# Row sums of a hash attention: the first three key tiles summed by transfers instead of GpSimd, with a new order of the work around them

## The chip, the cores and the metric

One core of a Trainium2 chip. The metric is the time of one launch on the device in microseconds (us), as the median of several runs. A program on one core has no second core to compare with, so a run's state is judged by its distance from the fastest run of the same kernel. Ratios are the mean time of one kernel's fast runs over that of the kernel before in the same rounds, with a 95% interval, so not quite the ratio of the medians quoted beside them.

Engines: PE is TensorE (matmuls; PEld its weight loads), DVE VectorE, ACT ScalarE, POOL GpSimd, SP SyncE, which issues most transfers. `L694` is line 694 of the kernel.

## The reference, cut to what matters

```python
q, k, v: (4, 8, 768, 64) float32        # batch, heads, sequence, head dimension
q_bits = einsum(q, proj) > 0             # 6 hash bits a row, the same for k
mask   = bucket(q_bits)[..., :, None] == bucket(k_bits)[..., None, :]
scores = where(mask, q @ k.T / 8, -1e9)
attn   = exp(scores - max);  attn = attn / (attn.sum(-1) + 1e-9)
x      = (attn @ v) as (3072, 512)
h      = x @ w_in                        # 512 -> 2048
out    = (max(h, 0) + alpha * min(h, 0)) @ w_out      # 2048 -> 512
```

The argument is about `attn.sum(-1)`, the row sums.

## The kernel before

Attention is done in 32 units: 16 pairs of heads, two halves of 384 queries each. A unit has six key tiles; for each, PE makes the scores transposed (keys on partitions), ACT takes the exponential into a tile `p(u, kc)` of 128 x 2 x 384 floats, and PE multiplies it with v. The sum over keys is a sum over the six tiles, then over partitions: GpSimd adds tiles 0, 1 and 2 to `accp`, DVE adds tiles 3, 4, 5 and `accp` to `accd`, and a matmul with ones (`totals`) sums `accd` over the partitions, for DVE to divide by. In the same 32 units, DVE pre-processes the weights of the feed-forward part.

```python
    def add_first(u):
        accp[u] = pool.tile([P, 2, CW], F32, name=f"accp{u}", tag="accp")
        do(POOL.tensor_tensor(accp[u], p(u, 0), p(u, 1), op=ALU.add))

    def add_third(u):
        do(POOL.tensor_tensor(accp[u], accp[u], p(u, 2), op=ALU.add))

    def add_last(u):
        accd[u] = pool.tile([P, 2, CW], F32, name=f"accd{u}", tag="accd", bufs=1)
        do(DVE.tensor_tensor(accd[u], p(u, 3), p(u, 4), op=ALU.add))
        do(DVE.tensor_tensor(accd[u], accd[u], p(u, 5), op=ALU.add))
        do(DVE.tensor_tensor(accd[u], accd[u], accp[u], op=ALU.add))
    ...
    for u in range(UNITS):
        scores(u, 0)                 # key tiles 0 and 1
        add_first(u)
        if u > 0:
            add_last(u - 1)
        ...                          # first turn (transposes of q) or first half of the hashes
        if u > 0:
            attend(u - 1, 0)
        weight_parts(u)
        scores(u, 1)                 # key tiles 2 and 3
        add_third(u)
        weight_sum(u)
        weight_group(u)              # in every 4th (later every 2nd) unit: four sums and their stores
        ...                          # second turn (k), or second half of the hashes
        if u > 0:
            attend(u - 1, 1)
            totals(u - 1)
        scores(u, 2)                 # key tiles 4 and 5
        if u > 0:
            divide(u - 1)
        ...                          # loads; at u == 16 also x loads and GpSimd's four subtractions
```

`do` keeps the written order on each engine.

## Time and profile before

| | before |
|---|---|
| time, median of the runs told with the changed kernel | 997.8 us (997.5 to 998.2) |
| attention stage, to the start of its last exponential | 400.7 us |
| two undisturbed units | 23.62 us |

The prediction below shows the page's head and reads it. The groups of the sum (columns: line, engine, operation, out<-in, forms, count, then busy us, mean ns of one, idle time before and who ended it):

```profile
L667 POOL TENSOR_TENSOR accp<-pt,pt 128x768 f32<-128x768 f32 x32 | 62.0, 1939 | 222.5 <-ACT pt L658 185.2
...
L670 POOL TENSOR_TENSOR accp<-accp,pt 128x768 f32<-128x768 f32 x32 | 62.3, 1946 | 39.0 <-ACT pt L658 38.9
...
L676 DVE TENSOR_TENSOR accd<-accd,accp 128x768 f32<-128x768 f32 x32 | 53.4, 1667 | 3.3
...
L675 DVE TENSOR_TENSOR accd<-accd,pt 128x768 f32<-128x768 f32 x32 | 43.7, 1364 | 3.3
L674 DVE TENSOR_TENSOR accd<-pt,pt 128x768 f32<-128x768 f32 x32 | 40.3, 1260 | 0.0
```

The GpSimd additions are 62.0 + 62.3 us, 1.94 us each. The three DVE additions do the same amount of work each and should take the same time; they differ (1260, 1364, 1667 ns) because they are held up.

### The profile page before, as it was taken

What the parts mean: (1) busy time and instruction counts of PE and PEld (TensorE: products, weight loads), DVE (VectorE), ACT (ScalarE), POOL (GpSimd) and SP (SyncE); (2) the same over time, 40 slices, a digit from 0 to 9 for tenths busy, and PEclk for the clock granted to TensorE, in tenths of its full rate; (3) what the DMA queues carried; (4) which work ended last, traced back from release to release, by engine and by line L of the source; (5) the groups of instructions that cost most, each with busy time, mean ns of one, the idle gap of its engine ahead of it and who ended that gap; (6) DMA issues with size and microseconds to landing.
All of it is one profiled execution on the core that took longest, in us unless ns stands there. A gap on an engine that the chain in (4) does not pass through costs nothing.

```text
span 998.3 us, 12489 instructions
## 1 busy us (share of the span) xinstructions
PE 963.2 (96%) x4741; PEld 594.0 (60%) x4741; DVE 605.8 (61%) x959; ACT 371.0 (37%) x669; POOL 158.5 (16%) x98
## 2 busy tenths in 40 slices
PE   6999999989999998999999999999999999999997
PEld 3444444434444443455788655888656888556886
DVE  3999999999999999766600366500467300665100
ACT  6777676665777664222100122100222000222000
POOL 2333333262333333000300000300000300000000
PEclk9999999998999999999999999999999999999999
DMA  7465756355444431463400133300224200231000
GB/s 199 126 182 143 237 154 179 107 164 157 143 143 143 127 111 53 200 259 110 137 22 22 58 111 99 123 22 21 71 88 155 68 22 22 84 111 37 22 22 24
DMA packets 93316, 106.81 MB, mean 107 GB/s; under 512 B 53296, under 2 KB 79936, under 8 KB 93248
## 3 DMA queue, kind: packets, MB, share of 16 engines
q1 hardware_dynamic: 91680, 105.54, 33.1%
q8 instruction: 39, 0.64, 0.3%
q10 hardware_dynamic: 1568, 0.39, 0.2%
q14 instruction: 29, 0.24, 0.1%
HBM read 78.65 MB, written 27.26 MB: 106 GB/s over the span
## 4 chain that ended last, share of the span: by engine, by line
PE 61%; DVE 35%; ACT 1%; issue 1%; DMA 1%; DVEq 0%; SPq 0%; ACTq 0%
PE z_2a L756 6%; PE z_1a L756 6%; PE z_0a L756 6%; DVE accd L676 5%; DVE accd L675 4%; DVE accd L674 4%; DVE wx L553 3%; PE z_1c L756 3%; PE z_0c L756 3%; PE z_2c L756 3%; DVE wr L577 2%; DVE wr L557 2%; PE f_2a L756 2%; PE f_3a L756 2%; PE f_7a L756 2%; PE f_6a L756 2%
## 5 line engine op out<-in xcount | busy, mean ns | idle before, releaser
L658 ACT ACTIVATE pt<-sc 128x768 f32<-128x768 f32 x192 | 149.9, 813 | 119.8 <-PE sc L653 119.8
L653 PE MATMUL sc<-qT,kT 64*128 64x384 f32 x768 | 157.5, 487 | 0.0
L686 PE MATMUL av<-pt,vn 128*64 128x385 f32 (+1 forms) x768 | 138.1, 495 | 0.0
L667 POOL TENSOR_TENSOR accp<-pt,pt 128x768 f32<-128x768 f32 x32 | 62.0, 1939 | 222.5 <-ACT pt L658 185.2
L686 PEld LDWEIGHTS av<-pt,vn 128*64 128x64 f32 x768 | 49.4, 136 | 72.6 <-issue 72.6
L732 POOL TENSOR_TENSOR x<-x,x 128x768 f32<-128x768 f32 x16 | 31.9, 2005 | 364.0 <-DMA x<-x_s 363.4
L810 DVE TENSOR_TENSOR g<-g,g 128x384 f32<-128x384 f32 x128 | 82.5, 665 | 2.2
L653 PEld LDWEIGHTS sc<-qT,kT 64*128 64x128 f32 x768 | 69.8, 190 | 15.3 <-issue 15.2
L653 PEld LDWEIGHTS <-kb 64*128 64x128 bf16 x384 | 24.4, 94 | 79.3 <-issue 62.7
L653 PE MATMUL sc<-qb,kb 64*128 64x384 bf16 x384 | 64.6, 329 | 5.6 <-ACT pt L658 5.6
L670 POOL TENSOR_TENSOR accp<-accp,pt 128x768 f32<-128x768 f32 x32 | 62.3, 1946 | 39.0 <-ACT pt L658 38.9
L756 PE MATMUL z_2a<-wo,g 128*128 128x256 f32 x256 | 58.0, 379 | 0.5 <-ACT z_2u L763 0.5
L756 PE MATMUL z_1a<-wo,g 128*128 128x256 f32 x256 | 57.9, 379 | 0.0
L756 PE MATMUL z_0a<-wo,g 128*128 128x256 f32 x256 | 57.9, 379 | 0.0
L676 DVE TENSOR_TENSOR accd<-accd,accp 128x768 f32<-128x768 f32 x32 | 53.4, 1667 | 3.3
L803 DVE SCALAR_TENSOR_TENSOR g<-h,alpha 128x384 f32<-128x384 f32 x32 | 22.1, 692 | 54.4 <-ACT h L795 54.4
L756 PEld LDWEIGHTS z_2a<-wo,g 128*128 128x128 f32 x256 | 48.6, 190 | 8.1 <-ACT z_2u L763 0.9
L756 PEld LDWEIGHTS z_0a<-wo,g 128*128 128x128 f32 x256 | 48.6, 190 | 7.5
L756 PEld LDWEIGHTS z_1a<-wo,g 128*128 128x128 f32 x256 | 48.6, 190 | 6.6
L675 DVE TENSOR_TENSOR accd<-accd,pt 128x768 f32<-128x768 f32 x32 | 43.7, 1364 | 3.3
L674 DVE TENSOR_TENSOR accd<-pt,pt 128x768 f32<-128x768 f32 x32 | 40.3, 1260 | 0.0
L639 ACT ACTIVATE qb<-hs,hb 32x384 bf16<-32x384 f32 x64 | 36.7, 574 | 2.2 <-PE hs L636 1.0
(217 smaller groups left out, 1477.1 us busy)
## 6 DMA issues: line engine op xcount, KB each, us to landing
wi<-w_in_s SPq DMA_DIRECT2D x32, 896.0 KB, 4.6
raw<-in_moe_w_in_dram SPq DMA_DIRECT2D x16, 512.0 KB, 4.1
raw<-in_moe_w_out_dram SPq DMA_DIRECT2D x16, 512.0 KB, 3.6
w_in_s<-wsi SPq DMA_DIRECT2D x16, 448.0 KB, 5.4
w_out_s<-wso SPq DMA_DIRECT2D x8, 896.0 KB, 4.4
wo<-w_out_s SPq DMA_DIRECT2D x8, 896.0 KB, 7.4
qn<-in_q_dram SPq DMA_DIRECT2D x32, 192.0 KB, 3.7
vn<-in_v_dram SPq DMA_DIRECT2D x16, 384.0 KB, 4.4
```

The source lines that it names most:

```text
L639: do(ACT.activation(bits["q", pi][D * s : D * s + 32, cols], ps[r], AF.Sign, bias=hb[r]))
L653: do(PE.matmul(sc[:, s, :CW], what["k", pi][r, ks], what["q", pi][r, qs], start=first, stop=not first,))
L658: do(ACT.activation(pt[:, :, :CW], sc[:, :, :CW], AF.Exp, scale=SCALE / DOWN))
L667: do(POOL.tensor_tensor(accp[u], p(u, 0), p(u, 1), op=ALU.add))
L670: do(POOL.tensor_tensor(accp[u], accp[u], p(u, 2), op=ALU.add))
L674: do(DVE.tensor_tensor(accd[u], p(u, 3), p(u, 4), op=ALU.add))
L675: do(DVE.tensor_tensor(accd[u], accd[u], p(u, 5), op=ALU.add))
L676: do(DVE.tensor_tensor(accd[u], accd[u], accp[u], op=ALU.add))
L686: do(PE.matmul(av[u][D * s : D * s + D, :w], nat["v", pi][:, s, kc * D : (kc + 1) * D], prob[u, kc][:, s, :w], start=(kc == 0), stop=(kc = ...
L732: do(POOL.tensor_tensor(x_m[b, to], x_m[b, a], x_m[b, c], op=ALU.subtract))
L756: do(PE.matmul(self.ps[bank], self.left(left, k), self.right(right, k), start=start and k == 0, stop=k == self.nk - 1, skip_group_check=no ...
L810: do(DVE.tensor_tensor(g_m[to, i], g_m[x, i], g_m[y, i], op=op))
```

## The change

Its intent: get the additions off GpSimd, since they hold DVE up, by letting transfers do them. A transfer copies tile 0 into `accp`, two more, issued from GpSimd, add tiles 1 and 2 on the way. The rest makes room and time: DVE's addition of `accp` is moved behind the first weight operations of the next unit, weight sums are made one (later two) to a unit instead of four at once, and the second turn is moved behind the last scores.

```diff
     def weight_group(i):
         ...
-        for to, a, c in sums4:
-            do(DVE.tensor_tensor(w[:, to], w[:, a], w[:, c], op=ALU.subtract))
-        ... stores
+        for x in sums4:
+            sums_due.append((one, x))
+        sums_due.append((store, ()))      # weight_sums(n) makes n of them
     def add_first(u):
         accp[u] = pool.tile([P, 2, CW], F32, name=f"accp{u}", tag="accp")
-        do(POOL.tensor_tensor(accp[u], p(u, 0), p(u, 1), op=ALU.add))
+        nc.sync.dma_start(accp[u], p(u, 0))
+        nc.gpsimd.dma_start(accp[u], p(u, 1), accum_op=ALU.add)
     def add_third(u):
-        do(POOL.tensor_tensor(accp[u], accp[u], p(u, 2), op=ALU.add))
+        nc.gpsimd.dma_start(accp[u], p(u, 2), accum_op=ALU.add)
     def add_last(u):
         ...
+    def add_total(u):
         do(DVE.tensor_tensor(accd[u], accd[u], accp[u], op=ALU.add))
@@ the loop over units
         weight_parts(u)
+        if u > 0:
+            add_total(u - 1)
         scores(u, 1)
         add_third(u)
         weight_sum(u)
+        weight_sums(1 if u < HW else 2)
         weight_group(u)
-        (second turn of k, or second half of the hashes)
         if u > 0:
             attend(u - 1, 1)
             totals(u - 1)
         scores(u, 2)
         if u > 0:
             divide(u - 1)
+        (second turn of k, or second half of the hashes)
-        if u == HW:                       # HW is 16: x loads, GpSimd's four subtractions
+        if u == HW + 2:
```

More of the change, by code (lines that the diff above doesn't have):

```diff
@@ L584, in weight_sum @@
         ))
+    sums_due = []
     def weight_group(i):
@@ L597, in weight_group, with one, store, weight_sums @@
             return
-        for to, a, c in sums4:
+        def one(to, a, c):
             do(DVE.tensor_tensor(w[:, to], w[:, a], w[:, c], op=ALU.subtract))
-        if i < HW:
-            c, kk = divmod(n, 2)
-            for ii in range(4):
-                nc.sync.dma_start(w_in_s[4 * c + ii][:, :, kk], w[:, :, ii])
-        else:
-            nc.sync.dma_start(w_out_s[n], w)
+        def store():
+            if i < HW:
+                c, kk = divmod(n, 2)
+                for ii in range(4):
+                    nc.sync.dma_start(w_in_s[4 * c + ii][:, :, kk], w[:, :, ii])
+            else:
+                nc.sync.dma_start(w_out_s[n], w)
+        for x in sums4:
+            sums_due.append((one, x))
+        sums_due.append((store, ()))
+    def weight_sums(count):
+        while sums_due and (count or sums_due[0][0].__name__ == "store"):
+            fn, x = sums_due.pop(0)
+            count -= fn.__name__ == "one"
+            fn(*x)
     def turn(pi, name, half):
@@ L893, in fast_path @@
         weight_sum(u)
+        weight_sums(1 if u < HW else 2)
         weight_group(u)
-        if more:
-            if g == 0:
-                turn(pi + 1, "k", 0)
-                turn(pi + 1, "k", 1)
-            else:
-                hash_bits(pi + 1, 1)
         if u > 0:
@@ L908, in fast_path @@
             divide(u - 1)
+        if more:
+            if g == 0:
+                turn(pi + 1, "k", 0)
+                turn(pi + 1, "k", 1)
+            else:
+                hash_bits(pi + 1, 1)
         load_weight(u + 3)
-        if u == HW:
+        if u == HW + 2:
             load_w(0)
@@ L928, in fast_path @@
     add_last(last)
+    add_total(last)
     attend(last, 1)
@@ L932, in fast_path @@
     divide(last)
+    weight_sums(4)
     attn.close()
```

## The prediction

> **What bounds the kernel now.** I read the page first (span, busy shares, the 40 slices), then the chain of waits, then PE's list of waits over the attention stage, then the timeline of two units in it, then a table of short stretches.
>
> ```profile
> span 998.3 us, 12489 instructions
> PE 963.2 (96%) x4741; PEld 594.0 (60%) x4741; DVE 605.8 (61%) x959; ACT 371.0 (37%) x669; POOL 158.5 (16%) x98
> ...
> PE   6999999989999998999999999999999999999997
> ...
> DVE  3999999999999999766600366500467300665100
> ...
> PE 61%; DVE 35%; ACT 1%; issue 1%; DMA 1%; DVEq 0%; SPq 0%; ACTq 0%
> ```
>
> Two stages: attention fills the first 16 slices (to about 402 us), the feed-forward part the rest. In the second stage PE is full and DVE is half idle, and the change doesn't touch its matmuls. In the first both PE and DVE stand at nines, and the chain's 35% of DVE lies there almost alone. So the question is which of the two sets the pace. PE's waits from 18 to 410 us answer it:
>
> ```profile
> PE sm L698 <- DVE accd L676: 7.7, 6, 3.0
> PE sc L653 <- ACT pt L658: 5.6, 31, 0.4
> PE tp_q L614 <- DVE st L708: 2.7, 6, 0.6
> PE tp_k L614 <- ACT qT L615: 1.3, 1, 1.3
> PE hs L636 <- DVE st L708: 0.4, 1, 0.4
> ```
>
> In all 17.7 us of 392. PE is the bound even here, and DVE is nearly level with it: it stops PE in a few units only. Units are 32; the starts of the scores that open a unit in the timeline (128.81, 140.63, 152.45) are 11.82 us apart, and in that unit PE's rows follow each other without a gap but for one of 0.17 before those scores. All periods taken that way are 11.8 except: three of about 12.6 in the first half, each after a unit that makes four weight sums; five of 12.2 to 12.6 in the second half (303.22 to 315.82, for example), also by units with four sums; and one of 17.75.
>
> Why DVE is so full is seen in the timeline:
>
> ```profile
> 120.44 0.96 DVE L675 TENSOR_TENSOR accd<-accd,pt 128x768 f32<-128x768 f32 x1
> ...
> 120.64 2.44 POOL L667 TENSOR_TENSOR accp<-pt,pt 128x768 f32<-128x768 f32 x1 [6.32 <-ACT pt L658]
> ...
> 121.51 2.39 DVE L676 TENSOR_TENSOR accd<-accd,accp 128x768 f32<-128x768 f32 x1
> ```
>
> The same addition of 128x768 takes DVE 0.96 us alone and 2.39 beside a GpSimd addition. The groups say the same: accd rows mean 1260, 1364 and 1667 ns, the shift (L553) 1149 ns where it takes 430 alone.
>
> The 17.75 us unit:
>
> ```profile
> 210.37 8.39 POOL L732 TENSOR_TENSOR x<-x,x 128x768 f32<-128x768 f32 x4
> ...
> 212.68 2.19 DVE L557 SCALAR_TENSOR_TENSOR wr<-raw,wr 128x512 f32<-128x512 uint32 x1
> ...
> 225.84 1.55 PE L698 MATMUL sm<-accd,ones 128*64 128x384 f32 x4 [3.04 <-DVE accd L676]
> ```
>
> and the stretch after it (columns: PE, PEld, DVE, ACT, POOL busy, PEclk, DMA share, GB/s):
>
> ```profile
> 226.00:232.00 6.00, 6.00 (x22) 2.72 (x23) 5.66 (x14) 2.00 (x3) 0.00 (x0) 0.50 0.30 74
> ```
>
> Four GpSimd subtractions in a row hold four DVE operations at about 2.2 us where they take 0.7 (0.43 one of them): 6 us lost. PE then waits 3.4 us, and the last row (PEclk 0.50) shows it at half clock for the next 6 us or more, about 3 us more.
>
> **What the Trainium skill says.**
> 1. "SBUF — State Buffer", Who interferes with whom: GpSimd's only SBUF ports are DVE's second pair; a DVE operation with two SBUF inputs, or in a two-port mode, and a GpSimd operation that reads SBUF exclude each other for a whole instruction. The trace agrees: 0.96 against 2.39 us.
> 2. "DMA: Bandwidth & Descriptors", SWDGE vs HWDGE vs iDMA: a transfer that adds can be issued from GpSimd only, whose cores write the descriptors. Its Anatomy of one DMA puts some 2 us fixed on each. No adding transfer is in this trace; plain ones land after 3.1 (192 KB) to 4.4 us (384 KB), which fits.
> 3. "Collectives: The Full Stack", The bandwidth ceiling: an adding transfer reads two sources and so ran at half a copy's rate. No run shows it here yet.
> 4. "TensorE: Matmul & The Clock Gate", What's actually happening: the clock is halved after an idle window, judged in free-running windows of about 3.4 us. The half clock after the 3.04 us wait agrees; after a wait of 2.06 us at 384 there was none, so the phase matters.
>
> **The change part by part.**
> *GpSimd additions out.* 64 of them, 124 us busy, leave GpSimd; DVE loses what they held it up. By rows that ran alone, in start-to-start distances, a unit needs of DVE: three additions 3.15, five weight operations on 128x512 and the reduction 3.8, division 2.3, one weight sum 0.7 (two small ones 0.9), together 10.0 to 10.3 us. Against PE's 11.8 this is 1.5 to 1.8 us of room where there was none. The gain is not these microseconds of DVE, only PE's waits that they caused.
> *Weight sums spread.* One per unit (two small ones in the second half) in place of four at once. With the room above, the long periods go: 3 x 0.8 + about 3.6 in the second half = 6.0 us.
> *Second turn behind the scores.* Two transposes of k, or the second half of the hashes (0.8 us of PE), now lie between the last scores of a unit and the first of the next. The 0.17 us wait for the exponential of two tiles back is then covered: up to 31 x 0.17 = 5.3, of which I count 5.0. It also brings the sums' matmul 0.8 us earlier, and ACT does the copies ahead of the first exponentials: these come some 0.3 to 0.9 us later. No matmul is added or removed.
> *Loads and GpSimd subtractions two units later.* The 8.4 us of lock stay. With DVE's lead over the sums' matmul still about 2.2 us, PE waits some 3 us again; only the two GpSimd additions right after are gone. I count 2 us of the 6.
> *The end.* The last two units have no turns, so PE needs only about 10.1 us each; before, it waited 2.06 (384 us), 1.21 (397) and 1.09 (408). DVE is no longer late there, but the transfers have less time. I count 1 us.
> *Transfers added.* Per unit one copy of 393 KB and two additions of 393 KB onto it, one after another. DMA load: 256 packets of 1536 B at about 72 ns is 18 engine-us for the copy; at twice that, 37 for each addition: together 92 engine-us, or 5.8 us of all 16 engines in 11.7, 49%. The table of stretches shows 0.43 to 0.59 in the first half now. So the engines come near to full there, about 90% after.
> *Is the sum in time?* The first exponential of a unit ends some 3.4 us after its scores begin; the sum is due when the DVE addition before the next unit's sums' matmul must start, 11.7 + 7.1 = 18.8 us after. That leaves 15 us. I estimate copy 3.5, additions 5 each (2 fixed, 2.3 moved, 0.7 descriptors): 13.5. It fits, by 1.5 us.
> Sum: 6.0 + 5.0 + 2 + 1 = 14 us, 997.6 to about 984, if the chain of transfers is in time everywhere.
>
> **The rivals.**
> *The transfers become the wait.* If an addition takes 6.5 us and not 5, the chain needs 16.5, and as the budget grows by just what the unit grows, every unit becomes 1.5 us longer: 31 x 1.5 = 46 us slower, less the gains. Landings of 4.4 us for plain loads and the load on the engines speak for it; against it, that the addition was moved behind the weight's first operations, as one who had seen such a wait would do, and that GpSimd's transfers have a ring of their own. I give 30%: 995 to 1030 us. A milder form, only in the three or four units that also store weight sums (bursts at 0.9 of the engines in the slices), costs 3 us each: about 995.
> *PE was the bound, nothing comes.* If the excess periods have another cause, or the half clock falls in elsewhere (3 us each time), gains shrink to the 0.17s: about 992. The 96% of PE speak for a small effect; the long periods right at weight sums speak against none.
> *DVE's relief counts in full.* DVE's 124 us beside GpSimd can't be won: PE's waits are 17.7 us, with the half clock some 21. Even taking all of it gives 977, just 2%. So faster by over 2% is nearly shut out.
>
> **Range and chances.** 70% for the good case about 984 (978 to 992), 30% for the late chain (992 to 1030). Middle 987; 8 in 10 from 978 to 1009. Faster by over 2% means under 977.6: 4%. Slower by over 2% means over 1017.5: 11%. Within: 85%.
>
> **What would show it.** Right: the accd rows and the shift at about 0.95 and 0.43 us in the attention stage; units all 11.6 to 11.7 us apart; no wait of the sums' matmul for accd but near the four subtractions; DMA share 0.9 in the first half. Wrong: idle DVE before the third accd row with a DMA as releaser, or PE waiting for accd in every unit (late chain); the 0.17 gap still there (the turn covers nothing); DVE rows still at 2 us while GpSimd writes descriptors (a lock by another door); or a feed-forward stage whose length differs from 596 us, since I take it as untouched.

## More of the kernel before

The tiles `p` lie in a ring of ten buffers.

A table of one stretch of 23.15 us (about two units), with the busy time of each engine, then PE's granted clock, the share of the DMA engines and GB/s:

```profile
core 0: us, PE busy (x) PEld busy (x) DVE busy (x) ACT busy (x) POOL busy (x), PEclk, DMA share, GB/s
...
316.30:339.45 23.15, 22.49 (x152) 9.79 (x150) 22.04 (x34) 15.46 (x27) 7.97 (x4) 1.00 0.50 154
```

DVE is busy for 22.04 of 23.15 us, PE for 22.49.

## The result, and the profile after

The changed kernel took 1054.88 us in the median (1049.95 to 1060.54, 4 runs) against 997.81: ratio 1.0574 (1.0516 to 1.0632). It is 57 us slower, where the prediction said 987 with a range to 1009. It computes the right result.

The page of the changed kernel, the lines that answer to those shown of before:

```profile
span 1050.7 us, 12553 instructions
...
PE 978.2 (93%) x4741; PEld 596.5 (57%) x4741; DVE 524.1 (50%) x959; ACT 372.1 (35%) x669; POOL 111.3 (11%) x98
...
PE   6998989598879889999999999999999999999997
...
DVE  3666656466676767767660046630166600466100
...
PEclk9999999899979989999999999999999999999999
DMA  8888979879977987758330012410023400121000
...
PE 66%; DMA 21%; DVE 5%; issue 3%; ACT 3%; POOL 1%; SPq 0%; POOLq 0%; ACTq 0%; DVEq 0%
```

PE's busy time rose by 15.0 us (963.2 to 978.2) though it does the same 4741 matmuls, and its idle time from 998.3 - 963.2 = 35.1 to 1050.7 - 978.2 = 72.5, by 37.4. Together that is the whole difference of the two profiled spans, 52.4 us. It lies in the attention stage, whose last exponential now starts at 453.7 us, 53.0 later; the feed-forward part is as long as it was. DVE, at nines before, is mostly at sixes and sevens: what the change set out to relieve is relieved. The row PEclk has eights and a seven in the attention stage: half clock. It is where the 15 us of longer matmuls come from: in the attention stage PE is busy for 39.5 us at half clock, before for 9.5, and half of the 30.0 more is 15.0. And the chain, once a third DVE's, has DMA at 21%.

PE's and the others' waits in the attention stage (columns: engine, line, what it waited for, us in total, times, longest):

```profile
DVE accd L694 <- DMA accp<-pt: 109.8, 25, 12.7
POOL accp L686 <- DMA accp<-pt: 109.5, 23, 7.0
...
PE sm L716 <- DVE accd L694: 51.0, 18, 10.7
...
PE sc L668 <- ACT pt L673: 2.8, 3, 2.4
```

The matmul of the sums waits 51.0 us for DVE's `accd`, DVE waits 109.8 us for the transfers into `accp`, and GpSimd, which only issues them, waits 109.5 us at the second addition for the first to land. So it is one chain: copy, first addition, second addition, DVE's addition, matmul. The scores' wait for an exponential is down to 2.8 us in three places, from 5.6 in 31: the moved turn does what it was meant to.

One unit of it in the timeline (start, duration, engine, line, operation; in brackets the idle time before and who ended it). Its tile 0 was ready at 118.83:

```profile
123.18 0.63 SPq L682 DMA_DIRECT2D accp<-pt  x1
...
128.41 1.20 POOL L683 DMA_DIRECT2D accp<-pt  x1 [8.11 <-DVE rc L728]
...
134.91 1.20 POOL L686 DMA_DIRECT2D accp<-pt  x1 [5.31 <-DMA accp<-pt]
...
141.76 0.96 DVE L694 TENSOR_TENSOR accd<-accd,accp 128x768 f32<-128x768 f32 x1 [7.72 <-DMA accp<-pt]
142.00 1.20 POOL L683 DMA_DIRECT2D accp<-pt  x1 [5.89 <-DMA accp<-pt]
...
142.78 0.87 PE L716 MATMUL sm<-accd,ones 128*64 128x384 f32 x4 [3.81 <-DVE accd L694]
...
143.75 1.44 PE L668 MATMUL sc<-qT,kT 64*128 64x384 f32 x4
```

The copy is issued 4.35 us late, because SP's queue, which issues in order, stood for 5.2 us behind a load of x that waited for a store. The first addition is issued 5.2 us after it, the second 6.5 us after that, and DVE, which had waited 7.72 us, gets the sum at 141.76, 22.9 us after the tile was ready. PE had waited 3.81 us, and of the scores that follow, four matmuls take 1.44 us in place of 0.81. At 142.00 the next unit's first addition is issued, its copy having landed: two chains overlap.

The group of DVE's last addition, and the transfers (queue: packets, MB, share of 16 engines; issues: KB each, median us from issue to landing):

```profile
L694 DVE TENSOR_TENSOR accd<-accd,accp 128x768 f32<-128x768 f32 x32 | 31.0, 968 | 109.8 <-DMA accp<-pt 109.8
```

```profile
q0 software_dynamic: 17408, 25.17, 14.3%
...
accp<-pt POOLq DMA_DIRECT2D x64, 384.0 KB, 5.6
```

`software_dynamic` is the queue of the transfers that GpSimd issues. The additions' packets of 1536 bytes took 146 ns each in the mean, the copy's 75. DVE's last addition takes 0.97 us now, where it took 1.67, and DVE sits idle for 109.8 before it. An addition lands 5.6 us after its issue in the median, and its issue holds GpSimd for 1.20 us (the POOL rows of the timeline).

From the trace I measured each unit's chain, from the end of the exponential that makes tile 0 to the end of the last packet of the second addition. It takes 17.8 us in the mean, 16.7 in the median and 13.6 to 27.4 in single units. Its parts in the mean: 0.7 until the copy is issued, 5.3 from there to the issue of the first addition, 6.3 to the issue of the second, 5.5 to its landing. The shortest of each anywhere are about 0, 3.3, 4.9 and 4.0. Of the 18 waits of PE for a sum, 14 stand in even units (39.9 of the 51.0 us): in undisturbed units (those of run 10 below) an even unit's sum is due 14.8 us after tile 0 is ready, an odd one's 15.8, counted to 1.02 us before the sums' matmul, which is DVE's last step. And a wait for an even unit's sum gives the next chain, already under way, that much more time.

### The profile page after: what moved, and what is told of

Read it like the earlier page. It is cut to its first block, busy times and chain, and to the rows that moved or that the text cites. A ratio compares the mean times of both kernels' runs of the same rounds, so it can differ in the third digit from the quotient of the medians.

```text
span 1050.7 us, 12553 instructions
## 1 busy us (share of the span) xinstructions
PE 978.2 (93%) x4741; PEld 596.5 (57%) x4741; DVE 524.1 (50%) x959; ACT 372.1 (35%) x669; POOL 111.3 (11%) x98
## 3 DMA queue, kind: packets, MB, share of 16 engines
q0 software_dynamic: 17408, 25.17, 14.3%
## 4 chain that ended last, share of the span: by engine, by line
PE 66%; DMA 21%; DVE 5%; issue 3%; ACT 3%; POOL 1%; SPq 0%; POOLq 0%; ACTq 0%; DVEq 0%
DMA accp<-pt 20%; PE z_2a L774 5%; PE z_1a L774 5%; PE z_0a L774 5%; PE sc L668 5%; PE z_2c L774 3%; PE z_1c L774 3%; PE z_0c L774 3%; PE av L704 2%; PE f_2a L774 2%; PE f_3a L774 2%; PE f_0a L774 2%; PE f_7a L774 2%; PE f_6a L774 2%; PE f_5a L774 2%
## 5 line engine op out<-in xcount | busy, mean ns | idle before, releaser
L668 PE MATMUL sc<-qT,kT 64*128 64x384 f32 x768 | 166.0, 512 | 0.0
L668 PEld LDWEIGHTS sc<-qT,kT 64*128 64x128 f32 x768 | 73.1, 200 | 23.3 <-issue 23.3
L694 DVE TENSOR_TENSOR accd<-accd,accp 128x768 f32<-128x768 f32 x32 | 31.0, 968 | 109.8 <-DMA accp<-pt 109.8
L716 PE MATMUL sm<-accd,ones 128*64 128x384 f32 x128 | 30.8, 562 | 51.0 <-DVE accd L694 51.0
L683 POOL DMA_DIRECT2D accp<-pt x32 | 39.0, 1220 | 203.9 <-DMA accp<-pt 58.8
L668 PEld LDWEIGHTS <-kb 64*128 64x128 bf16 x384 | 19.7, 96 | 71.5 <-issue 59.1
L686 POOL DMA_DIRECT2D accp<-pt x32 | 38.4, 1201 | 161.9 <-DMA accp<-pt 109.5
L716 PEld LDWEIGHTS sm<-accd,ones 128*64 128x64 f32 x128 | 8.1, 146 | 68.1 <-DVE accd L694 49.8
```

What stands on the lines that cost most here:

```text
L668: do(PE.matmul(sc[:, s, :CW], what["k", pi][r, ks], what["q", pi][r, qs], start=first, stop=not first,))
L683: nc.gpsimd.dma_start(accp[u], p(u, 1), accum_op=ALU.add)
L686: nc.gpsimd.dma_start(accp[u], p(u, 2), accum_op=ALU.add)
L716: do(PE.matmul(sums[u][D * s : D * s + D], ones, accd[u][:, s], start=True, stop=True))
```

## The experiments

The theory after the result: the three transfers, one behind the other, come later than the sum is due, and PE waits, and then runs at half clock. The rivals: the new order alone costs the time; the load on the DMA engines does, through other transfers and buffers; DVE is still too slow. Fourteen kernels were run, three rounds each, in five calls, so each call's kernel before is its own (997.9, 998.0, 999.2, 999.7 and 999.7 us).

| sum of tiles 0 to 2 made by | old order | new order |
|---|---|---|
| GpSimd | 997.8 (before) | 1008.9 |
| three transfers | 1077.7 | 1054.9 (the change) |
| copy and one addition by transfer, one by DVE | | 990.9 |
| one addition by DVE, one by transfer | 1009.3 | 979.5 |
| DVE alone | 986.1 | 978.2 |

The rest tells how this table was filled.

**1. The new order without the transfers.** GpSimd's two additions are put back, all else of the change is kept.

```diff
-        nc.sync.dma_start(accp[u], p(u, 0))
-        nc.gpsimd.dma_start(accp[u], p(u, 1), accum_op=ALU.add)
+        do(POOL.tensor_tensor(accp[u], p(u, 0), p(u, 1), op=ALU.add))
     ...
-        nc.gpsimd.dma_start(accp[u], p(u, 2), accum_op=ALU.add)
+        do(POOL.tensor_tensor(accp[u], accp[u], p(u, 2), op=ALU.add))
```

> The changed kernel with its transfers undone: GpSimd adds the first three tiles again, while spread weight sums, second turn behind the scores, the late third addition and the later loads stay. Theory (the transfers' chain is late): the loss is gone and the order keeps its gains, some 988 us (983 to 996), PE's waits for accd under 8 us, the slow accd rows (over 1.2 us in the mean) back. Rival (the new order itself costs time): 1010 us or more.

Measured: 1008.85 us, ratio 1.0108 (1.0092 to 1.0125). A miss, close to the rival's 1010: with GpSimd's additions the order is not a gain, it costs 11 us. PE's waits in the attention stage:

```profile
PE sm L715 <- DVE accd L693: 13.5, 14, 2.7
...
PE tp_k L629 <- DVE st L725: 9.0, 11, 5.7
```

With DVE as full as before, the sums' matmul, which now comes 0.8 us earlier, waits in 14 units, and the second turn, now behind it, waits for a buffer in PSUM (the memory that takes PE's results) that DVE's division frees. Still this is 46 us from the changed kernel: the order is not the cause of the loss.

**2. Nobody waits for the sum.** All transfers are issued as in the change, but DVE adds tile 2 in place of `accp`, so that nothing reads what they make. The result is wrong.

```diff
     def add_total(u):
-        do(DVE.tensor_tensor(accd[u], accd[u], accp[u], op=ALU.add))
+        do(DVE.tensor_tensor(accd[u], accd[u], p(u, 2), op=ALU.add))
```

> The changed kernel with all three transfers of each unit still issued, but the last addition reads a tile of probabilities in place of their sum, so nobody waits for it (the result is wrong on purpose). Theory (latency of the chain): 984 us (980 to 992), DMA share in attention still 0.8 or more, hardly any half clock. Rival (the load on the DMA engines: other transfers come late, the queue is blocked): 1020 us or more, with PE, ACT or DVE waiting for q, k, v or weight loads.

Measured: 1000.75 us (995.84 to 1002.8), ratio 1.0032 (1.0009 to 1.0056). So waiting for the sum is 54 of the changed kernel's microseconds, and that settles the main question. But it is not 984 either:

```profile
ACT pt L673 <- DMA accp<-pt: 21.1, 9, 4.3
...
PE sc L668 <- ACT pt L673: 15.6, 11, 3.9
```

PE waits for ACT and ACT for transfers: the exponentials find the buffers of the ring not yet read out. Late transfers cost even when no one needs what they bring, 17 us here by the expectation, 21 against the one-transfer kernel of run 6, though that has a DVE addition more in each unit. This run also shows the three transfers near the pace that the prediction counted on: the DMA share is 1.01 and 1.06 in the two stretches from 293.15 to 339.45 us, where 0.9 was foretold, and the chain takes 20.4 us in the mean.

**3. The sum due later.** The sums' matmul and the division are moved behind the last scores and the second turn, DVE's addition behind the weight sums: some 2.7 us more time for the chain by the count made before the run, the same transfers.

```diff
         weight_parts(u)
-        if u > 0:
-            add_total(u - 1)
         ...
         if u > 0:
+            add_total(u - 1)
             attend(u - 1, 1)
-            totals(u - 1)
         scores(u, 2)
-        if u > 0:
-            divide(u - 1)
         (second turn, or second half of the hashes)
+        if u > 0:
+            totals(u - 1)
+            divide(u - 1)
```

> The changed kernel with the sums' matmul moved behind the unit's last scores and the turn after them, and the third addition behind the weight sums: the chain has about 2.7 us more per unit, bytes and results are the same. Theory: of the chains that were late by a median of 1.7 us and a mean of 2.8, most are now in time; PE's wait for accd falls from 51 us to 10 to 25, and the half clock with it; 1000 us (990 to 1025). Rival (DMA load): no change, 1045 to 1060.

Measured: 1025.39 us, ratio 1.0254 (1.0218 to 1.0291), 0.4 above the theory's range and far from the rival's.

```profile
DVE accd L694 <- DMA accp<-pt: 36.2, 19, 7.4
...
PE sm L716 <- DVE accd L694: 26.5, 9, 8.1
```

Nine waits for `accd` are left of 18, and 26.5 us of 51.0. Giving the chain some 2.7 us more won 29.5 us, with the bytes unchanged and the chains no shorter (19.1 us in the mean): what is missing is time for the chain.

**4. Only a copy and one addition.** The second adding transfer is left out, DVE adds tile 2.

```diff
     def add_third(u):
-        nc.gpsimd.dma_start(accp[u], p(u, 2), accum_op=ALU.add)
+        pass
     def add_total(u):
+        do(DVE.tensor_tensor(accd[u], accd[u], p(u, 2), op=ALU.add))
         do(DVE.tensor_tensor(accd[u], accd[u], accp[u], op=ALU.add))
```

> The changed kernel with the copy and one adding transfer only; DVE adds the third tile itself (a fourth addition of 1.05 us, 11.1 to 11.3 us of DVE per unit). The chain is one addition (5 to 6 us) shorter, the result is right. Theory: chain 11.5 us against a budget of 15, PE waits for accd only near the subtractions and at the end; 988 us (982 to 1000). Rival (DMA load): the load falls from 49% to 29% on top of the others, so also faster but with waits left, 1010 to 1030.

Measured: 990.91 us (989.88 to 991.97), ratio 0.993 (0.9914 to 0.9947). As expected, and ahead of both kernels. DVE has an addition more here than in the change, so the rival that DVE is too slow is out as well. Two units take 23.15 us where nothing disturbs them. Three waits for the total are left, at 123.6 (1.05 us), 171.2 (4.98) and 247.4 us (4.33), the last two with half clock after them.

**5. The transfers in the old order.** The kernel before with the three transfers in place of GpSimd's additions (the two lines of run 1, the other way round) and nothing else.

> The kernel before with the three transfers in place of GpSimd's two additions and nothing else of the change. Theory (the transfers' chain comes too late, whatever the order): the chain stays near 17 us, the sums' matmul is only about 0.8 us later than in the changed kernel, so 1045 us (1030 to 1065), with PE's wait for the total above 30 us. Rival (the loss is a product of the transfers and the new order, which asks for the sum 0.8 us sooner and puts the total behind the weights' parts): below 1020 us.

Measured: 1077.74 us, ratio 1.0798 (1.078 to 1.0816). The theory's side, and worse than it said; the new order is worth 23 us with transfers in place.

```profile
DVE accd L677 <- DMA accp<-pt: 142.8, 18, 19.2
...
PE sm L699 <- DVE accd L677: 58.4, 16, 13.8
```

In the old order DVE's addition of `accp` stands at the start of the next unit, ahead of the weight operations. DVE waits there for the transfers (142.8 us, once 19.2), and everything behind it is late too. Moving the addition back was part of the change for a reason.

**6. One addition by DVE, one by transfer.** No copy: DVE adds tiles 0 and 1 after the weight sum, one transfer adds tile 2.

```diff
     def add_first(u):
         accp[u] = pool.tile(...)
-        nc.sync.dma_start(accp[u], p(u, 0))
-        nc.gpsimd.dma_start(accp[u], p(u, 1), accum_op=ALU.add)
     def add_third(u):
+        do(DVE.tensor_tensor(accp[u], p(u, 0), p(u, 1), op=ALU.add))
         nc.gpsimd.dma_start(accp[u], p(u, 2), accum_op=ALU.add)
     ...
-        add_third(u)
         weight_sum(u)
+        add_third(u)
```

> The changed kernel with no copying transfer and one adding transfer: VectorE adds the first two tiles, the transfer adds the third, VectorE the rest (four additions on VectorE as in the run with the third tile on VectorE, but one transfer less a unit). Theory (latency of the chain and load of the DMA engines): 985 us (982 to 989), PE's wait for the total below 3 us in sum, DMA share of the attention stage about 0.1 below that of the run with a copy and one addition. Rival (VectorE at four additions a unit is the next bound, or the one transfer issued later than the pair is late too): 990 us or more, with PE's wait for the total above 8 us.

Measured: 979.51 us (978.58 to 981.31), ratio 0.9816 (0.98 to 0.9833): better than the theory's range, because 985 was taken from the undersized gain of the prediction (below). 

```profile
PE sm L715 <- DVE accd L693: 1.3, 2, 0.8
```

PE waits 1.3 us for the total in all. One transfer is in time; the DMA share over two units is 0.73, where the run with a copy and one addition had 0.83 in the same stretch.

**7. Run 4 with GpSimd's subtractions spread.** The four subtractions that prepare x are made one to a unit from u = 19 on, not in a row.

```diff
-            sums_x(0)
+        if HW + 3 <= u < HW + 7:
+            sums_x(0, slice(u - HW - 3, u - HW - 2))
```

> The run with the third tile on VectorE, with GpSimd's four subtractions of the feed-forward one to a unit instead of four in a row. Theory (the stall at 247 us there, 4.33 us and half clock after it, comes from the adding transfer that GpSimd can't issue while it subtracts for 8.4 us): that stall goes, 4 to 6 us less: 985.5 us (984 to 988). Rival (the stall there comes from the x loads on the DMA engines): no change, 990 to 992.

Measured: 990.46 us, ratio 0.9933: no change, as the rival said, but not for the rival's reason either. The stall at 247 us is gone and others have come, two of them at 262.6 and 289.3 us, in the units of the subtractions:

```profile
259.99 3.00 DVE L582 SCALAR_TENSOR_TENSOR wso<-raw,wr 128x512 uint32<-128x512 uint32 x1
260.16 2.27 POOL L751 TENSOR_TENSOR x<-x,x 128x768 f32<-128x768 f32 x1
...
264.33 0.55 PE L629 MATMUL tp_k<-ident,kn 128*128 128x128 f32 x3 [1.78 <-DVE st L727]
```

A DVE operation that takes 0.69 us alone takes 3.00 beside the subtraction, the division is late, and the transposes wait 1.78 us for their PSUM buffer, with half clock after it. Run 4 shows the same there: from 241.4 us on, four DVE operations take 1.92 to 2.64 us each while GpSimd subtracts, and DVE's addition of `accp` at 250.71 waited for nothing. Not the transfer stood behind the subtractions; DVE did. Both theories of this run fell.

**8. The whole change without two accidents.** The copy issued from ACT's queue, so that it does not stand behind others in SP's, and the subtractions spread as in run 7.

```diff
-        nc.sync.dma_start(accp[u], p(u, 0))
+        nc.scalar.dma_start(accp[u], p(u, 0))
```

> The whole change, with two of its accidents removed: the copy is issued from ScalarE's queue instead of SyncE's, where it stands behind transfers that wait (0.71 us in the mean, up to 5.7), and GpSimd's four subtractions are spread one to a unit. Theory (the chain is late by its own length under load, the accidents are the smaller part): the mean chain falls from 17.8 to 16.5 us and the time to 1038 us (1022 to 1050), PE's wait for the total above 25 us. Rival (the accidents make the loss; the undisturbed chain of 13.5 us fits): 1005 us or less.

Measured: 1053.52 us, ratio 1.0563 (1.0526 to 1.0599). Outside the theory's range too: the mean chain is 17.4 us in place of 17.8 (one profiled execution of each, so the difference is not shown) and the time is unchanged. PE still waits 45.6 us for the total. The rival, that accidents make the loss, is out.

**9. The whole change without the loads of q, k and v.** All pairs of heads use the first pair's tiles (wrong result).

```diff
     def load(pi, name, queue=None):
+        if pi > 0:
+            nat[name, pi] = nat[name, 0]
+            return
     def magnitude(pi, name):
-        do(ACT.activation(t, t, AF.Square, accum_out=...))
+        do(ACT.activation(squares[name], t, AF.Square, accum_out=...))     # t is needed again
```

> The whole change, with q, k and v of the first pair used for all pairs, so that 590 KB of loads a unit leave the DMA engines (wrong result on purpose; all computation stays). Theory (other transfers on the same engines stretch the three transfers of the sum): the mean chain falls from 17.8 us to 15 or less, and the time to 1005 us (985 to 1025). Rival (the chain stretches itself, since it is longer than the 10.5 or 12.6 us from one unit to the next and two chains share the engines and GpSimd's queue): mean chain above 16.5 us and 1035 us or more.

Measured: 1036.95 us, ratio 1.0364 (1.0316 to 1.0412), mean chain 17.1 us. On the rival's side in both numbers, though 18 us are won.

**10. All five additions on DVE.** Run 6 with its one transfer made a DVE addition: no transfer and no GpSimd in the sum.

```diff
     def add_third(u):
         do(DVE.tensor_tensor(accp[u], p(u, 0), p(u, 1), op=ALU.add))
-        nc.gpsimd.dma_start(accp[u], p(u, 2), accum_op=ALU.add)
     def add_total(u):
+        do(DVE.tensor_tensor(accd[u], accd[u], p(u, 2), op=ALU.add))
         do(DVE.tensor_tensor(accd[u], accd[u], accp[u], op=ALU.add))
```

> The run with a VectorE sum and one transfer, with that transfer too made a VectorE addition: five additions of 0.95 us a unit on VectorE, no transfer and no GpSimd in the sum. Theory (VectorE was full only because GpSimd's additions stretched its own; without them it has 19.9 us of work in 23.15 in the one-transfer run, and 1.9 more still fit): 980 us (978 to 984), two units in 23.15 us. Rival (at 21.8 of 23.15 us VectorE is late for the sums' matmul in every unit): 990 us or more, with PE waiting for the total in most units.

Measured: 978.19 us (977.89 to 979.1), ratio 0.9792 (0.9776 to 0.9808), with run 6 the fastest of all, and the right result; whether it is 2% stays unclear, as the interval holds 0.98. The table of the stretch shown of before:

```profile
316.30:339.45 23.15, 23.15 (x158) 10.16 (x160) 21.79 (x40) 17.05 (x29) 0.00 (x0) 1.00 0.42 137
```

PE has no idle time left in the stretch. DVE makes five additions a unit and is busy for 21.79 us in two; before, it made three and was busy for 22.04 in the same time. Four additions of 0.95 us are 3.8 us more, so the three-addition work of two units alone is 18.0, and at least 4.0 us of before were spent being held up (there two units take 24.4 us, so the stretch holds less than their whole work). GpSimd's two additions saved DVE two additions a unit and cost it at least as much again.

**11. One DVE addition and one transfer in the old order.** Run 6's sum in the kernel before.

> The kernel before with only the sum changed as in the one-transfer run (VectorE adds the first two tiles, one transfer the third), the old order of weight sums, turns and totals kept. Theory (VectorE's relief gives most, the order only the 0.17 us gaps before the scores, some 5 us): 985 us (981 to 990). Rival (the order is what gives the gain, as VectorE with four weight sums at once is late): 992 us or more. Second rival (the order gives nothing once VectorE has room): 979 to 981.

Measured: 1009.26 us, ratio 1.0101 (1.0075 to 1.0128): the first rival's side. But not because weight sums are late:

```profile
DVE accd L676 <- DMA accp<-pt: 62.0, 28, 7.8
```

DVE waits for the transfer in 28 units, 62.0 us, at the start of each unit as in run 5, and what follows is late.

**12. All five on DVE in the old order.** The last cell of the table: the kernel before with run 10's sum.

> The kernel before with all five additions on VectorE, in the old order: no transfer and no GpSimd in the sum. It completes the table of old and new order by who makes the sum. Theory (the one-transfer run in the old order was slow, 1009 us, because VectorE waits for the transfer at the start of a unit, ahead of the weights; without a transfer nothing waits there): 985 us (981 to 992), with the 0.17 us gaps before the scores left. Rival (in the old order a full VectorE, with its weight sums four at once, delays the turns whoever makes the sum): 995 us or more.

Measured: 986.13 us, ratio 0.9868 (0.9852 to 0.9885), where the theory put it. With no transfer at the start of the unit, hardly anything is late even with four weight sums at once: PE waits 0.9 us for the total in all. Two units take 23.62 us here and 23.15 in run 10; over 31 units that is 31 x 0.235 = 7.3 us, nearly all of the 7.9 between the two. From start to start, PE's scores take 4.40 us a unit here and 4.15 in run 10, and its other matmuls about the same: the difference stands at the scores, which is where the moved turn should help. But the turn was moved alone in no run, so this is the worth of the new order, and the turn's share of it is argued.

**13. Transfers in even units only.** Odd units sum on DVE as in run 10, so each chain of transfers has no neighbour.

```diff
     def add_first(u):
+        if u % 2 == 0:
             nc.sync.dma_start(accp[u], p(u, 0))
             nc.gpsimd.dma_start(accp[u], p(u, 1), accum_op=ALU.add)
     ...                      # likewise the third; odd units as in run 10
```

> The changed kernel with the three transfers in even units and five VectorE additions in odd units, so that each chain of transfers has the engines and GpSimd's queue to itself as far as sums go. Theory (the chain stretches itself: being longer than a unit it runs beside the next unit's): the mean chain of the even units falls from 17.8 to 14.5 us or less, and the time to 985 us (978 to 995). Rival (each chain is late for reasons of its own, other loads or GpSimd's late first packets): mean chain above 16 us and half the loss left, 1010 us or more.

Measured: 1032.28 us, ratio 1.0323 (1.0301 to 1.0344), mean chain of the even units 17.0 us. The rival's side: a chain alone is nearly as late as one with a neighbour (17.7 in the change's even units), and the even units alone bring 54 of the 77 us that lie between the change and run 10. These are the units whose sum is due sooner, so as much can't be assumed of the odd ones.

**14. The whole change without nearly two thirds of the other transfers.** Run 9, and also without all but three of the raw weight loads (wrong result).

```diff
     def load_weight(i):
+        if i >= 3:
+            raw[i] = raw[i % 3]
+            return
```

> The whole change without the loads of q, k and v (576 KB a unit) and without all but the first three of the raw weight loads (512 KB a unit): 1088 of the 1728 KB a unit that the other transfers move (wrong result on purpose). Theory (the other transfers together stretch the chain: the time in which the packets of an addition move rises with the share that others take, correlation 0.87 in the changed kernel): mean chain 14.5 us or less, 1000 us (985 to 1015). Rival (the chain is stretched by what the other transfers have no part in, late first packets after GpSimd's issue and waits in its own order): mean chain above 16 us, 1025 us or more.

Measured: 1010.83 us, ratio 1.012 (1.0104 to 1.0137); mean chain 15.3 us, median 14.3.

```profile
PE sm L725 <- DVE accd L703: 22.8, 10, 7.3
```

The time is in the theory's range, the mean chain between the two sides, its median on the theory's. In this run no chain under 15.5 us stopped PE (but for one of 13.6 at the very end, where units have no turns and are shorter), and from 284 to 391 us, where they take 12.4 to 15.5, PE never waits. The 44 us against the whole change are the load of 1088 KB a unit. What is late still are three units whose copy stood in SP's queue for 6.8 us or whose first addition came 11 to 12 us after the copy (13.8 of the 22.8 us), and six with steps of 6 to 8 us. So other transfers are the main part of what stretches the chain. The loads of q, k and v alone (run 9) are not enough; those of the weights were not left out alone.

## Why the prediction was wrong

The failed step is "Is the sum in time?". It put the chain at copy 3.5 and additions of 5 each, 13.5 us, against 15 us until the sum is due, and read "It fits, by 1.5 us".

- The 15 us held: the sum is due after 14.8 and 15.8 us in turn in run 10, and in run 14 no chain under 15.5 us stopped PE, but for one at the very end.
- The 13.5 us are the chain of an undisturbed unit: run 14's quiet units take 12.4 to 14.5, its additions 4.9 to 5.0 from issue to issue, as estimated. In the changed kernel the chain takes 17.8 us in the mean. At the pace of run 2, near the one foretold, it takes 20.4. The prediction had computed a DMA load near full, and then taken each transfer's time as if nothing else ran. A hint was at hand: plain loads of 384 KB landed after 4.4 us, which it read as fitting, though the fit that it names gives 2.9 (last section). By runs 8, 9, 13 and 14 the excess of some 4 us has no single source: 0.4 for the blocked queue and the subtractions, 0.7 for the loads of q, k and v, 0.8 for the neighbouring chain, 2.5 for q, k, v and the weights together. Each is the difference of two profiled executions; only the last is large enough to rest on.
- The rival "The transfers become the wait" was the right one; it was given 30% and then capped at 1030. Its 46 us of waiting, for 51.0 measured, are near by luck: it had every unit wait 1.5 us for a chain of 16.5. The mean chain is 17.8, which by its rule makes 31 x 2.8 = 87 us, but only 18 units wait, 2.8 us each, since a wait for one sum gives the next chain time too. The half clock was known from the profile of before and not put into this rival: it stands behind nine of the ten waits of 2 us and more, and is the 15.0 us by which PE's busy time grew.
- The bytes' load was sized right: 37 engine-us (us of one of the 16 DMA engines) for each addition; the software queue's share of 14.3% of 1050.7 us over 32 units is 4.7 us of all engines a unit, against 2 x 37 / 16 = 4.6. The share that the engines had before was not: 0.43 to 0.59 is that of two single units, while the stretches of 25 us from 18 to 218 us have 0.45 to 0.69, in the mean 0.57. With the 0.49 added, this makes over 1.0 and not 0.9, which is what run 2 shows. That the addition takes twice a copy's packet time was right too: 146 ns a packet against 75.
- DVE's relief came as told: 0.95 to 0.97 us for each addition.
- The good case of 984 was undersized. With the sum in time (runs 6 and 10) it is 978 to 979.5. The moved turn was counted as 5.0, and the new order, of which it is a part, is worth 7.3 (run 12), and the stall at the subtractions, of which 2 us of 6 were counted, is nearly gone when DVE has the room (0.79 us of PE's in run 6).
- The rival "DVE's relief counts in full" put a floor of 977 under everything; run 10 with 978.2 stands on it.

What stays open: additions began to move 1.76 us after their issue at the least, 2.5 in the mean and up to 4.6. Part of it goes with the load (2.0 in the mean in run 14), and part may be DVE: over the 64 additions of the changed kernel the delay goes with the time of DVE's transposes in those first 1.76 us (correlation 0.52), but in run 14, with the same DVE work, not at all. No run separates these.

## What to carry to other kernels

A chain of dependent transfers has to be timed under the load of the stage in which it will run, with the spread of its steps, and not as the sum of best cases: a margin of a tenth on 15 us is none. Before moving work from one engine to a third, try it on the engine that seems full: here DVE was full because of GpSimd's help, and taking the help away (two additions back on DVE, with the changed order) won about 2%, where transfers lost 6%. And put an instruction that waits for a slow producer as far back in its engine's order as its consumer allows: the same order that won 23 us with transfers, and 8 us with DVE's own sum, lost 11 with GpSimd's.

## What the Trainium skill lacked or had wrong

- "DMA: Bandwidth & Descriptors", Anatomy of one DMA, fits a transfer as 2.0 us and its bytes over 436 GB/s: 2.9 us for 393 KB. No page has the time of an adding transfer from SBUF to SBUF. Here it holds GpSimd 1.20 us at its issue, its first packet starts 1.76 us or more after that issue began, and the next one that depends on it is issued 4.9 us after it at the least and 6.3 in the mean.
- "TensorE: Matmul & The Clock Gate", Why this matters for your kernels, advises against idle gaps of PE over some 3 us. In the changed kernel PE waits of 2.01 and 2.29 us were followed by half clock of 3.4 us, a wait of 2.88 us was not, and none of those under 2 us was; in run 7 a wait of 1.78 us was. A gap of 2 us, or a little less, is already at risk.
